# Two cached-attention decode problems on one core: V loads moved from SyncE's to ScalarE's DMA queue, half sums relayed through GpSimd

## The chip, the core and the metric

The kernel runs on one core of a Trainium2 chip. A core has a matmul engine (TensorE, "PE" in the profile, with its weight loads shown apart as "PEld"), an elementwise and reduction engine (VectorE, "DVE"), an activation engine (ScalarE, "ACT"), a general engine (GpSimd, "POOL") and an engine that only issues transfers and waits (SyncE, "SP"). The engines run their own instruction streams and meet at semaphores. Transfers between the large memory (HBM) and the on-chip memory (SBUF) are done by 16 DMA engines; an instruction on SP or ACT starts a transfer ("SPq" and "ACTq" are their issuing sides in the profile). The metric is the device time of one execution in microseconds.

## The reference, cut to what matters

Two independent problems, A and B, are computed and their results concatenated. Each has one query token `x` of width 512, 32 heads of width 128, and a key and a value cache of 16384 positions in bf16; A attends to all positions, B to the last 4096.

```python
def one(x, k_cache, v_cache, wq, wo):            # B first cuts k_cache, v_cache to the last W = 4096 keys
    q = (x @ wq).reshape(B, Sq, 32, 128).transpose(0, 2, 1, 3)
    scores = einsum("bhqd,bhkd->bhqk", q, k_cache) * 128 ** -0.5
    p = softmax(scores, axis=-1)
    o = einsum("bhqk,bhkd->bhqd", p, v_cache)
    return o.transpose(0, 2, 1, 3).reshape(B, Sq, 32 * 128) @ wo     # wo: 4096 x 512
out = concatenate([one(A...), one(B...)], axis=-1)
```

Every key and value is used once, so the bytes are fixed: A's caches are 2 x 134.2 MB, B's parts of them 2 x 33.6 MB, and the four weight matrices 4.19 MB each.

## The kernel before, in words

The work is cut into 20 *loads*. A load is 8.39 MB of K and the same 8.39 MB of V: for A two heads (16 loads, numbers 0 to 15), for B eight heads (4 loads, 16 to 19), in two halves `u` of four heads, each its own transfer of 4.19 MB (`st.U` is 1 for A and 2 for B). One of the 128 partitions receives one contiguous row of HBM from a transfer: 64 KB for an A load, 32 KB for half a B load.

There are two K buffers (`kt`, slots 0 and 1, `_slot(i)` alternates) and one V buffer (`vt`). At the start `vt` holds both query weight matrices, and slot 0 of `kt` small scratch tiles; at the end `vt` takes both output weight matrices, and the last V load (19) goes into the K slot of load 18.

For each load i the engines do this:

- VectorE (`_vector_program`): `mult` multiplies K in place by the query (L292); then `scores(i-1)` sums the 8 remaining partial columns that TensorE left of the load before (L306) into `sc`; then `add` adds the two halves of the head dimension (L300) and signals `s_add`; then `pick(i-1)` cuts the wanted blocks out of the PV product of the load before (L320, L322, L327).
- TensorE (`_tensor_program`): `red(slot)` sums with identity matmuls over the halved head dimension into `red`, four banks, each bank taking one count of `s_add` and giving one of `s_red`; then `pv` multiplies probabilities with V into `acc`, for each half once its probabilities (`s_p`) and its V half are there, giving one count of `s_pv`; then it waits for `pick` and adds the result to `f`. Then comes the next load.
- ScalarE (`_scalar_program`): exponentials of `sc` into `p`, one per head (L216).

So `exp(i)` comes after `scores(i)`, which stands on VectorE behind `mult(i+1)`: the probabilities of a load need the K of the next load. Loads 0 and 1 are cut in four and two parts on VectorE, so that TensorE starts earlier.

SP issues all large transfers, in one written-out order (`_sync_program`, L128): both query weights, K0, then K1, V0, K2, V1, K3, V2 and so on to K19, V18, V19, then the output weights in seven pieces (two of 2.1 MB for A; 2.1, 1.05, 0.52, 0.26, 0.26 MB for B). K(i) first waits until load i-2 has left its slot (`s_red`); V(i-1) until `pv(i-2)` has left `vt` (`s_pv`); V19 until slot of load 18 is free; the output weights until `pv(18)`. ScalarE's queue carries only the two 1 KB rows of x, at the start.

After load 15, and after load 19, `norm` divides by the softmax sums and places the result as columns. After the last norm, TensorE multiplies with A's output weights, then with B's; VectorE and ScalarE convert the output rows, and SP stores them.

Of the kernel before, what the change touches and what calls it, by code (L numbers as in the profile page):

```python
# [19 lines left out]
KEYS = 256  # L20
NB = 4
# [98 lines left out]
def _slot(i):  # L120
    return (i + 1) % 2
# [3 lines left out]
    return cx.p[u][:, 0 : st.keys * st.R].rearrange("p (t g e) -> p t g e", g=st.R, e=4)  # L125


def _sync_program(nc, cx, loads):  # L128
    e = nc.sync
    stA, stB = cx.sts  # L130
    for st in cx.sts:
        st.s_wq.on(e.dma_start(out=st.wq_t, in_=st.wq.rearrange("(p c) f -> p c f", c=st.KC)), 16)

    def kv(st, i, which):
        j = i if st is stA else i - stA.L
        view = st.k_view if which == "k" else st.v_view
        last = which == "v" and i == len(loads) - 1
        for u in range(st.U):
            h0 = (j * st.U + u) * st.R
            k0 = u * st.keys  # L140
            if which == "k":
                out = cx.kt[:, _slot(i), k0 : k0 + st.keys, :]
                sem = cx.s_k[_slot(i)][u]
            elif last:
                out = cx.kt[:, _slot(i - 1), k0 : k0 + st.keys, :]
                sem = cx.s_vlast[u]
            else:
                out = cx.vt[:, k0 : k0 + st.keys, :]
                sem = cx.s_v[u]
            ins = e.dma_start(out=out, in_=view[h0 : h0 + st.R].rearrange("g (i l) d -> i g l d", l=st.keys))  # L150
            sem.on(ins, 16)

    pv = 0
    kv(loads[0], 0, "k")
    for i in range(1, len(loads)):
        if i == 1:
            cx.s_q.wait(e, stA.N // stA.R // 512 + stB.N // stB.R // 512)
        else:
            cx.s_red.wait(e, NB * (i - 1))
        kv(loads[i], i, "k")  # L160
        if i > 1:
            pv += loads[i - 2].U
            cx.s_pv.wait(e, pv)
        kv(loads[i - 1], i - 1, "v")
    n = len(loads)
    cx.s_red.wait(e, NB * (n - 1))
    kv(loads[-1], n - 1, "v")
    cx.s_pv.wait(e, pv + loads[-2].U)
    for st, j0, m, sem in cx.pieces:
        src = st.wo.rearrange("(p j) f -> p j f", j=st.J)  # L170
        sem.on(e.dma_start(out=st.wo_t[:, j0 : j0 + m, :], in_=src[:, j0 : j0 + m, :]), 16)  # L171
    for st in cx.sts:
        st.s_row.wait(e, len(st.out_at))
        cx.s_end.on(e.dma_start(out=cx.out[0, 0:1, st.at : st.at + st.DN], in_=cx.row[0:1, st.at : st.at + st.DN]), 16)
    cx.s_end.wait(e, 32)


def _pool_program(nc, cx):
    e = nc.gpsimd
    e.memset(cx.one[:, :], 1.0)  # L180
    e.memset(cx.ones_col[:, :], 1.0)
    cx.s_own.on(e.memset(cx.ones, 1.0))
    cx.s_own.wait(e, 1)
    cx.s_pool.on(e.affine_select(
        out=cx.ident[:, :], in_=cx.ones[:, 0:P], pattern=[[-1, P]], compare_op=ALU.is_equal,
        fill=0.0, base=0, channel_multiplier=1,
    ))
    w = cx.place_at + 2 * P
    cx.s_pool.on(e.affine_select(
        out=cx.place[:, :], in_=cx.ones[0 : 2 * H, 0:w], pattern=[[1, w]], compare_op=ALU.is_equal,  # L190
        fill=0.0, base=-cx.place_at, channel_multiplier=-cx.n_r,
    ))


def _scalar_program(nc, cx, loads):
    e = nc.scalar
    stA, stB = cx.sts
    for w, st in enumerate(cx.sts):
        st.s_x.on(e.dma_start(out=cx.row[0:1, w * st.D : (w + 1) * st.D], in_=st.x[0, 0:1, :]), 16)
    n = 0  # L200
    for st in cx.sts:
        m = st.N // st.R // 512
        n += m
        cx.s_q.wait(e, n)
        st.s_qall.on(e.copy(st.qall[:, :], cx.red[:, 0:m, :].rearrange("p j f -> p (j f)")))
    cx.s_dve.wait(e, cx.n_off)
    for i, st in enumerate(loads):
        if i == stA.L:
            _orow(e, cx, stA)
        cx.s_sc.wait(e, i + 1)  # L210
        j = i if st is stA else i - stA.L
        for u in range(st.U):
            p = _p_view(cx, st, u)
            for g in range(st.R):
                h = st.f_at + (j * st.U + u) * st.R + g
                ins = e.activation(  # L216
                    out=p[:, :, g, :],
                    in_=cx.sc[:, u * st.keys : (u + 1) * st.keys].rearrange("p (t e) -> p t e", e=4),
                    func=ACT.Exp, scale=SCALE, bias=st.off[:, g : g + 1], accum_out=cx.cs[:, h : h + 1],
                )  # L220
            cx.s_p.on(ins)
    _orow(e, cx, stB)
    w = stB.DN // 2
    stB.s_o.wait(e, 1)
    stB.s_row.on(e.copy(cx.row[0:1, stB.at + w : stB.at + 2 * w], cx.out_ps(stB)[1]))
# [10 lines left out]
def _vector_program(nc, cx, loads):  # L236
# [4 lines left out]
    def did(ins):  # L241
        return own.on(ins)

    for st in cx.sts:
        did(e.memset(st.xb_flat, 0.0))
        did(e.memset(st.sel[:, :], 0.0))
    for acc in cx.acc:
        cx.n_acc = did(e.memset(acc[:, :], 0.0))
    n = did(e.memset(cx.zero, 0.0))
    cx.n_zero = n  # L250
    cx.s_pool.wait(e, 1)
    ident = cx.ident[:, :]
    n = did(e.tensor_reduce(out=cx.rows, in_=ident.rearrange("p (c w) -> p w c", w=H), axis=AX.X, op=ALU.add))
    own.wait(e, n)
# [41 lines left out]

    def add(i, k0, k1, n):
        k = cx.kt[:, _slot(i), k0:k1, :]
        own.wait(e, n)
        cx.s_add.on(e.tensor_tensor(  # L300
            out=k[:, :, 0 : DH // 2], in0=k[:, :, 0 : DH // 2], in1=k[:, :, DH // 2 : DH], op=ALU.add,
        ), NB * (k1 - k0) // KEYS)

    def scores(i):
        cx.s_red.wait(e, NB * (i + 1))
# [30 lines left out]
        st.s_ocs.on(e.tensor_copy(st.oc[:, :], cx.oc_out(st)))  # L336

    for i, st in enumerate(loads):
        n = KEYS // (4, 2)[i] if i < 2 else KEYS
        if i in (0, stA.L):  # L340
            st.s_qall.wait(e, 1)
        for k in range(0, KEYS, n):
            m = mult(i, k, k + n)
            if i and k == 0:
                scores(i - 1)
            add(i, k, k + n, m)
        if i:
            pick(i - 1)
            if i == stA.L:
                norm(stA)  # L350
# [10 lines left out]
def _tensor_program(nc, cx, loads):  # L361
# [1 line left out]
    stA, stB = cx.sts  # L363
    mm = lambda *a, **k: e.matmul(*a, skip_group_check=True, **k)  # L364

    cx.s_pool.wait(e, 2)
    cx.s_dve.wait(e, cx.n_zero)
    mm(cx.f[0 : 2 * H, 0:DH], lhsT=cx.zero[:, 0 : 2 * H], rhs=cx.zero, start=True, stop=True)
    for w, st in enumerate(cx.sts):
        st.s_x.wait(e, 16)  # L370
# [98 lines left out]
@with_exitstack  # L469
def kernel(  # L470
    ctx: ExitStack,
    tc: tile.TileContext,
    A_x: bass.AP,
    A_k_cache: bass.AP,
    A_v_cache: bass.AP,
    A_wq: bass.AP,
    A_wo: bass.AP,
    B_x: bass.AP,
    B_k_cache: bass.AP,
    B_v_cache: bass.AP,  # L480
    B_wq: bass.AP,
    B_wo: bass.AP,
    out: bass.AP,
):
    nc = tc.nc
    SkA = A_k_cache.shape[2]
    SkB = B_k_cache.shape[2]
    WB = min(4096, max(256, SkB // 4))

    cx = _Ctx()  # L490
    cx.out = out
    cx.pe_only = bass.OrderedEngineSet([PE])
    stA = _problem(cx, "A", A_x, A_k_cache, A_v_cache, A_wq, A_wo, 0, SkA, 0)
    stB = _problem(cx, "B", B_x, B_k_cache, B_v_cache, B_wq, B_wo, SkB - WB, WB, A_wo.shape[1])
    cx.sts = (stA, stB)
    loads = [stA] * stA.L + [stB] * stB.L

    ctx.enter_context(tc.tile_critical(sync_engine=mybir.EngineType.SP))
    _alloc(nc, cx, ctx, stA, stB)
    sem = lambda name: _Sem(nc, ctx, name)  # L500
    for st in cx.sts:
        for name in ("wq", "x", "xT", "xb", "qall", "rows", "recip", "orow", "oc", "ocs", "o", "row"):
            setattr(st, f"s_{name}", sem(f"{name}{st.name}"))
    for name in ("q", "red", "pv", "own", "pool", "dve", "sc", "p", "add", "pick", "end"):
        setattr(cx, f"s_{name}", sem(name))
    cx.s_k = [[sem(f"k{a}{u}") for u in range(2)] for a in range(2)]
    for pair in cx.s_k:
        for s in pair:
            s.seen = 0
    cx.s_v = [sem(f"v{u}") for u in range(2)]  # L510
    cx.s_vlast = [sem(f"vl{u}") for u in range(2)]
    J = stA.J
    cx.pieces = [(stA, 0, J // 2, sem("woA0")), (stA, J // 2, J // 2, sem("woA1"))]
    j0 = 0
    for x in (J // 2, J // 4, J // 8, J // 16, J // 16):
        cx.pieces.append((stB, j0, x, sem(f"woB{j0}")))
        j0 += x
    cx.xT = lambda st: cx.oc_ps[:, 0 : st.KC]
    cx.oc_out = lambda st: cx.oc_ps[:, st.J * (st is stB) : st.J * (st is stB) + st.J]
    cx.out_ps = lambda st: [cx.red[r : r + 1, b, 0 : st.DN // len(st.out_at)] for r, b in st.out_at]  # L520

    _sync_program(nc, cx, loads)
    _pool_program(nc, cx)
    _vector_program(nc, cx, loads)
    _scalar_program(nc, cx, loads)
    _tensor_program(nc, cx, loads)


# [28 lines left out]
```

The softmax here doesn't subtract the row's maximum and nothing guards it: scores larger than these inputs give would overflow.

## Time and profile before

| | |
|---|---|
| median of 9 runs | 822.26 us (822.10 to 822.67) |
| the profiled execution's own time | 822.11 us |
| its span, from the first to the last instruction | 820.4 us |
| DMA | 352.42 MB, mean 430 GB/s |
| busy: VectorE | 603.5 us (74%) |
| busy: TensorE matmuls / weight loads | 336.4 us (41%) / 127.1 us (15%) |
| busy: ScalarE | 35.5 us (4%) |
| busy: GpSimd | 1.3 us (0%), all before 2.3 us |

The span is measured inside the device's time, which is 1.7 us longer in this execution. "Busy" counts computing instructions; for DMA the page gives a row of tenths over 40 equal slices of the span, with the rate in each slice under it. A row of the timeline reads: start, duration, engine, line, operation, output<-input, count, and in brackets the idle time of that engine just before and what ended it. "SPq" rows are the moments at which a transfer is issued, not its duration.

### The profile page before, as it was taken

To read this page: it belongs to the slowest core of one execution; us is meant where nothing else is said; L and a number is where in the kernel's file an instruction comes from. 1 tells how busy PE (TensorE), PEld (TensorE's weight loads), DVE (VectorE), ACT (ScalarE), POOL (GpSimd) and SP (SyncE) were. 2 spreads that over 40 slices of the span, in tenths; PEclk is the share of its full clock that TensorE was granted. 3 is DMA by queue.
4 is the path that set the end of the run, shared out by engine and by line. 5 is a ranking of instruction groups with operands and counts; after the bars stand their busy time and mean duration, and the time that the engine had idled before them with its cause. 6 is when DMAs were issued, how large, how long until landed. Compare 5 with 4: busy or idle time off the path is not lost. (4 is left out here: it accounts for less than half of the span.)

```text
span 820.4 us, 5948 instructions
## 1 busy us (share of the span) xinstructions
PE 336.4 (41%) x2149; PEld 127.1 (15%) x2149; DVE 603.5 (74%) x172; ACT 35.5 (4%) x134; POOL 1.3 (0%) x9
## 2 busy tenths in 40 slices
PE   3533347152424343252606071524343352616276
PEld 1211112020101111110202020201111120202022
DVE  2089995959595968768595959595959969696921
ACT  0100000000000000000000000000000001010110
POOL 0000000000000000000000000000000000000000
PEclk9855667595856666756758575858576776857589
DMA  9999999999999999999999999999999999999997
GB/s 384 435 457 412 457 412 457 412 457 413 454 415 454 415 454 412 457 412 457 412 457 413 454 415 451 419 444 425 441 428 423 446 423 423 433 435 435 433 431 317
DMA packets 8223, 352.42 MB, mean 430 GB/s; under 512 B 916, under 2 KB 920, under 8 KB 1304
## 3 DMA queue, kind: packets, MB, share of 16 engines
q1 hardware_dynamic: 8212, 352.33, 99.3%
q8 instruction: 4, 0.07, 0.0%
q14 instruction: 3, 0.02, 0.0%
q10 hardware_dynamic: 4, 0.00, 0.0%
HBM read 352.32 MB, written 0.00 MB: 429 GB/s over the span
## 5 line engine op out<-in xcount | busy, mean ns | idle before, releaser
L292 DVE TENSOR_TENSOR kt<-kt,qallA 128x32768 bf16<-128x32768 bf16 (+2 forms) x20 | 276.2, 13811 | 155.9 <-DMA kt<-in_A_k_cache_dram 155.9
L364 PE MATMUL acc<-vt,p 128*8 128x512 bf16 (+1 forms) x1216 | 110.1, 539 | 354.5 <-PEq L42 354.5
L364 PE MATMUL red<-kt,ident 128*128 x640 | 179.5, 448 | 40.4 <-PEq L42 40.4
L300 DVE TENSOR_TENSOR kt<-kt 128x16384 bf16<-128x16384 bf16 (+2 forms) x24 | 174.3, 7262 | 0.2
L364 PEld LDWEIGHTS acc<-vt,p 128*8 128x8 bf16 (+1 forms) x1216 | 36.6, 112 | 427.1 <-issue 418.2
L364 PEld LDWEIGHTS red<-kt,ident 128*128 128x128 bf16 x640 | 71.1, 111 | 145.3 <-issue 98.0
L292 DVE TENSOR_TENSOR kt<-kt,qallB 128x16384 bf16<-128x16384 bf16 x8 | 69.5, 8691 | 12.9 <-DMA kt<-in_B_k_cache_dram 12.9
L306 DVE TENSOR_REDUCE sc<-red 128x256 f32<-128x2048 f32 x20 | 45.7, 2284 | 8.0 <-PE red L364 8.0
L216 ACT ACTIVATE p<-sc,offA 128x256 bf16<-128x256 f32 x32 | 16.0, 500 | 602.6 <-DVE sc L306 602.6
L364 PE MATMUL f<-s,win 128*32 128x128 f32 x48 | 11.2, 322 | 63.6 <-PEq L42 63.6
L364 PE MATMUL red<-vt,kt 128*128 128x512 bf16 x64 | 18.1, 453 | 7.9 <-DMA vt<-in_A_wq_dram 5.9
L216 ACT ACTIVATE p<-sc,offB 128x128 bf16<-128x128 f32 x32 | 12.4, 388 | 113.2 <-DVE sc L306 113.2
L327 DVE TENSOR_REDUCE s<-acc 128x128 f32<-128x512 f32 x24 | 16.6, 691 | 0.8
L364 PEld LDWEIGHTS f<-s,win 128*32 128x32 f32 x48 | 4.3, 122 | 74.4 <-issue 74.1
L322 DVE TENSOR_TENSOR acc<-acc,maskA 128x512 f32<-128x512 f32 x16 | 11.1, 693 | 0.0
L320 DVE COPY win<-selB 128x32 f32<-128x32 f32 x8 | 1.4, 179 | 12.2 <-PE acc L364 12.2
L364 PEld LDWEIGHTS red<-vt,kt 128*128 128x128 bf16 x64 | 7.1, 113 | 18.6 <-issue 13.7
L364 PE MATMUL red<-vt,ocA 128*1 128x512 bf16 x32 | 7.2, 379 | 0.2 <-DMA vt<-in_A_wo_dram 0.2
L364 PE MATMUL acc<-kt,p 128*16 128x512 bf16 x64 | 5.3, 507 | 4.3 <-PEq L42 4.3
L320 DVE COPY win<-selA 128x32 f32<-128x32 f32 x16 | 2.8, 175 | 5.8 <-PE acc L364 5.8
L216 ACT ACTIVATION_READ_ACCUMULATOR p<-sc,offA 128x1 f32 x32 | 6.0, 187 | 0.0
L355 DVE CAST row<-red 1x512 bf16<-1x512 f32 x1 | 0.7, 679 | 7.2 <-PE red L364 7.2
(47 smaller groups left out, 40.4 us busy)
## 6 DMA issues: line engine op xcount, KB each, us to landing
kt<-in_B_k_cache_dram SPq DMA_DIRECT2D x8, 4096.0 KB, 35.4
vt<-in_B_v_cache_dram SPq DMA_DIRECT2D x6, 4096.0 KB, 28.7
kt<-in_B_v_cache_dram SPq DMA_DIRECT2D x2, 4096.0 KB, 38.3
vt<-in_A_wq_dram SPq DMA_DIRECT2D x1, 4096.0 KB, 12.1
vt<-in_B_wq_dram SPq DMA_DIRECT2D x1, 4096.0 KB, 21.3
vt<-in_A_wo_dram SPq DMA_DIRECT2D x2, 2048.0 KB, 23.3
vt<-in_B_wo_dram SPq DMA_DIRECT2D x1, 2048.0 KB, 29.8
vt<-in_B_wo_dram SPq DMA_DIRECT2D x1, 1024.0 KB, 31.8
```

The source lines that it names most:

```text
L216: ins = e.activation(out=p[:, :, g, :], in_=cx.sc[:, u * st.keys : (u + 1) * st.keys].rearrange("p (t e) -> p t e", e=4), func=ACT.Exp, sc ...
L292: n = did(e.tensor_tensor(out=k, in0=k, in1=q.rearrange("p (o d) -> p o d", o=1).broadcast_to([P, b - a, DH]), op=ALU.mult,))
L300: cx.s_add.on(e.tensor_tensor(out=k[:, :, 0 : DH // 2], in0=k[:, :, 0 : DH // 2], in1=k[:, :, DH // 2 : DH], op=ALU.add,), NB * (k1 - k0) ...
L306: cx.s_sc.on(e.tensor_reduce(out=cx.sc[:, :], in_=cx.red[:, :, :].rearrange("p b (k w) -> p (b k) w", w=W), axis=AX.X, op=ALU.add,))
L320: did(e.tensor_copy(cx.win[u][:, :], st.sel[:, at : at + H]))
L322: n = did(e.tensor_tensor(out=acc, in0=acc, in1=st.mask[:, :].rearrange("p (x o) -> p x o", o=1).broadcast_to([P, 4, DH]), op=ALU.mult,))
L327: cx.s_pick.on(e.tensor_reduce(out=cx.s[u][:, :], in_=acc.rearrange("p x d -> p d x"), axis=AX.X, op=ALU.add,))
L355: stA.s_row.on(e.tensor_copy(cx.row[0:1, 0 : stA.DN], cx.out_ps(stA)[0]))
L364: mm = lambda *a, **k: e.matmul(*a, skip_group_check=True, **k)
```

## The change

Five edits:

- All V loads are issued by ScalarE, on its own DMA queue; SP keeps the weights, the K loads and the output store. The common part becomes the function `_kv`. ScalarE's order for load i is: wait for `pv(i-1)` (for the last load: for `red(18)`, as before; for load 0: nothing), issue V(i), wait for `scores(i)`, exponentials. On SP, K(i) waits as before for `red(i-2)`, and nothing stands between two K loads any more. The output weights wait for `pv(18)` as before.
- The x rows, on ScalarE's queue as before, wait for the first of GpSimd's signals.
- GpSimd takes over from VectorE the zero fills of `xb`, `sel` and `zero`. VectorE and TensorE wait for the third signal of `s_pool`.
- `add` signals `s_half` by one; GpSimd waits for each and adds the 4, 2 or 1 counts to `s_add`. The first `add` of a load waits for `s_sc` instead of VectorE's own counter.
- The critical section is owned by GpSimd instead of SP: the other engines start, and the section ends, through GpSimd.

The output weights stay in the same pieces.

```diff
--- before.py
+++ after.py
@@ -125,47 +125,42 @@
     return cx.p[u][:, 0 : st.keys * st.R].rearrange("p (t g e) -> p t g e", g=st.R, e=4)
 
 
+def _kv(e, cx, loads, i, which):
+    st = loads[i]
+    stA = cx.sts[0]
+    j = i if st is stA else i - stA.L
+    view = st.k_view if which == "k" else st.v_view
+    last = which == "v" and i == len(loads) - 1
+    for u in range(st.U):
+        h0 = (j * st.U + u) * st.R
+        k0 = u * st.keys
+        if which == "k":
+            out = cx.kt[:, _slot(i), k0 : k0 + st.keys, :]
+            sem = cx.s_k[_slot(i)][u]
+        elif last:
+            out = cx.kt[:, _slot(i - 1), k0 : k0 + st.keys, :]
+            sem = cx.s_vlast[u]
+        else:
+            out = cx.vt[:, k0 : k0 + st.keys, :]
+            sem = cx.s_v[u]
+        ins = e.dma_start(out=out, in_=view[h0 : h0 + st.R].rearrange("g (i l) d -> i g l d", l=st.keys))
+        sem.on(ins, 16)
+
+
 def _sync_program(nc, cx, loads):
     e = nc.sync
     stA, stB = cx.sts
     for st in cx.sts:
         st.s_wq.on(e.dma_start(out=st.wq_t, in_=st.wq.rearrange("(p c) f -> p c f", c=st.KC)), 16)
 
-    def kv(st, i, which):
-        j = i if st is stA else i - stA.L
-        view = st.k_view if which == "k" else st.v_view
-        last = which == "v" and i == len(loads) - 1
-        for u in range(st.U):
-            h0 = (j * st.U + u) * st.R
-            k0 = u * st.keys
-            if which == "k":
-                out = cx.kt[:, _slot(i), k0 : k0 + st.keys, :]
-                sem = cx.s_k[_slot(i)][u]
-            elif last:
-                out = cx.kt[:, _slot(i - 1), k0 : k0 + st.keys, :]
-                sem = cx.s_vlast[u]
-            else:
-                out = cx.vt[:, k0 : k0 + st.keys, :]
-                sem = cx.s_v[u]
-            ins = e.dma_start(out=out, in_=view[h0 : h0 + st.R].rearrange("g (i l) d -> i g l d", l=st.keys))
-            sem.on(ins, 16)
-
-    pv = 0
-    kv(loads[0], 0, "k")
+    _kv(e, cx, loads, 0, "k")
     for i in range(1, len(loads)):
         if i == 1:
             cx.s_q.wait(e, stA.N // stA.R // 512 + stB.N // stB.R // 512)
         else:
             cx.s_red.wait(e, NB * (i - 1))
-        kv(loads[i], i, "k")
-        if i > 1:
-            pv += loads[i - 2].U
-            cx.s_pv.wait(e, pv)
-        kv(loads[i - 1], i - 1, "v")
-    n = len(loads)
-    cx.s_red.wait(e, NB * (n - 1))
-    kv(loads[-1], n - 1, "v")
-    cx.s_pv.wait(e, pv + loads[-2].U)
+        _kv(e, cx, loads, i, "k")
+    cx.s_pv.wait(e, sum(st.U for st in loads[:-1]))
     for st, j0, m, sem in cx.pieces:
         src = st.wo.rearrange("(p j) f -> p j f", j=st.J)
         sem.on(e.dma_start(out=st.wo_t[:, j0 : j0 + m, :], in_=src[:, j0 : j0 + m, :]), 16)
@@ -175,8 +170,13 @@
     cx.s_end.wait(e, 32)
 
 
+def _parts(i):
+    return (4, 2)[i] if i < 2 else 1
+
+
 def _pool_program(nc, cx):
     e = nc.gpsimd
+    stA, stB = cx.sts
     e.memset(cx.one[:, :], 1.0)
     e.memset(cx.ones_col[:, :], 1.0)
     cx.s_own.on(e.memset(cx.ones, 1.0))
@@ -190,11 +190,23 @@
         out=cx.place[:, :], in_=cx.ones[0 : 2 * H, 0:w], pattern=[[1, w]], compare_op=ALU.is_equal,
         fill=0.0, base=-cx.place_at, channel_multiplier=-cx.n_r,
     ))
+    for st in cx.sts:
+        e.memset(st.sel[:, :], 0.0)
+        e.memset(st.xb_flat, 0.0)
+    cx.s_pool.on(e.memset(cx.zero, 0.0))
+    n = 0
+    for i in range(stA.L + stB.L):
+        m = _parts(i)
+        for _ in range(m):
+            n += 1
+            cx.s_half.wait(e, n)
+            e.sem_inc(cx.s_add.h, NB // m)
 
 
 def _scalar_program(nc, cx, loads):
     e = nc.scalar
     stA, stB = cx.sts
+    cx.s_pool.wait(e, 1)
     for w, st in enumerate(cx.sts):
         st.s_x.on(e.dma_start(out=cx.row[0:1, w * st.D : (w + 1) * st.D], in_=st.x[0, 0:1, :]), 16)
     n = 0
@@ -207,6 +219,11 @@
     for i, st in enumerate(loads):
         if i == stA.L:
             _orow(e, cx, stA)
+        if i == len(loads) - 1:
+            cx.s_red.wait(e, NB * i)
+        elif i:
+            cx.s_pv.wait(e, sum(s.U for s in loads[:i]))
+        _kv(e, cx, loads, i, "v")
         cx.s_sc.wait(e, i + 1)
         j = i if st is stA else i - stA.L
         for u in range(st.U):
@@ -241,14 +258,9 @@
     def did(ins):
         return own.on(ins)
 
-    for st in cx.sts:
-        did(e.memset(st.xb_flat, 0.0))
-        did(e.memset(st.sel[:, :], 0.0))
     for acc in cx.acc:
-        cx.n_acc = did(e.memset(acc[:, :], 0.0))
-    n = did(e.memset(cx.zero, 0.0))
-    cx.n_zero = n
-    cx.s_pool.wait(e, 1)
+        did(e.memset(acc[:, :], 0.0))
+    cx.s_pool.wait(e, 3)
     ident = cx.ident[:, :]
     n = did(e.tensor_reduce(out=cx.rows, in_=ident.rearrange("p (c w) -> p w c", w=H), axis=AX.X, op=ALU.add))
     own.wait(e, n)
@@ -296,10 +308,13 @@
 
     def add(i, k0, k1, n):
         k = cx.kt[:, _slot(i), k0:k1, :]
-        own.wait(e, n)
-        cx.s_add.on(e.tensor_tensor(
+        if i and k0 == 0:
+            cx.s_sc.wait(e, i)
+        else:
+            own.wait(e, n)
+        cx.s_half.on(e.tensor_tensor(
             out=k[:, :, 0 : DH // 2], in0=k[:, :, 0 : DH // 2], in1=k[:, :, DH // 2 : DH], op=ALU.add,
-        ), NB * (k1 - k0) // KEYS)
+        ))
 
     def scores(i):
         cx.s_red.wait(e, NB * (i + 1))
@@ -336,7 +351,7 @@
         st.s_ocs.on(e.tensor_copy(st.oc[:, :], cx.oc_out(st)))
 
     for i, st in enumerate(loads):
-        n = KEYS // (4, 2)[i] if i < 2 else KEYS
+        n = KEYS // _parts(i)
         if i in (0, stA.L):
             st.s_qall.wait(e, 1)
         for k in range(0, KEYS, n):
@@ -363,8 +378,7 @@
     stA, stB = cx.sts
     mm = lambda *a, **k: e.matmul(*a, skip_group_check=True, **k)
 
-    cx.s_pool.wait(e, 2)
-    cx.s_dve.wait(e, cx.n_zero)
+    cx.s_pool.wait(e, 3)
     mm(cx.f[0 : 2 * H, 0:DH], lhsT=cx.zero[:, 0 : 2 * H], rhs=cx.zero, start=True, stop=True)
     for w, st in enumerate(cx.sts):
         st.s_x.wait(e, 16)
@@ -495,13 +509,13 @@
     cx.sts = (stA, stB)
     loads = [stA] * stA.L + [stB] * stB.L
 
-    ctx.enter_context(tc.tile_critical(sync_engine=mybir.EngineType.SP))
+    ctx.enter_context(tc.tile_critical(sync_engine=mybir.EngineType.Pool))
     _alloc(nc, cx, ctx, stA, stB)
     sem = lambda name: _Sem(nc, ctx, name)
     for st in cx.sts:
         for name in ("wq", "x", "xT", "xb", "qall", "rows", "recip", "orow", "oc", "ocs", "o", "row"):
             setattr(st, f"s_{name}", sem(f"{name}{st.name}"))
-    for name in ("q", "red", "pv", "own", "pool", "dve", "sc", "p", "add", "pick", "end"):
+    for name in ("q", "red", "pv", "own", "pool", "dve", "sc", "p", "add", "half", "pick", "end"):
         setattr(cx, f"s_{name}", sem(name))
     cx.s_k = [[sem(f"k{a}{u}") for u in range(2)] for a in range(2)]
     for pair in cx.s_k:
```

## The prediction

> **What bounds the kernel now.** I read the slices first, then the stretches of one load, the timeline of one load, and the end. The DMA row and the queue table of the page:
>
> ```profile
> DMA  9999999999999999999999999999999999999997
> GB/s 384 435 457 412 457 412 457 412 457 413 454 415 454 415 454 412 457 412 457 412 457 413 454 415 451 419 444 425 441 428 423 446 423 423 433 435 435 433 431 317
> ...
> q1 hardware_dynamic: 8212, 352.33, 99.3%
> ```
>
> The 16 DMA engines are never empty, so only the bytes count until the last piece. The same in two stretches of one A load each (columns: stretch, length, busy time of PE, PEld, DVE, ACT, POOL with counts, TensorE clock, DMA share, GB/s):
>
> ```profile
> 140.20:178.80 38.60, 15.31 (x103) 5.90 (x102) 29.41 (x7) 1.09 (x4) 0.00 (x0) 0.69 1.00 435
> 178.80:217.40 38.60, 14.08 (x101) 5.49 (x100) 29.39 (x6) 1.09 (x4) 0.00 (x0) 0.73 1.00 435
> ```
>
> 38.6 us for 16.78 MB is 434.7 GB/s: 19.3 us for one K or V load, and VectorE's 29.4 us fit inside. The page counts packets too: one per partition row explains them (32 A transfers, 16 of B, 9 of weights, 128 each, is 7296; 57 x 16 small ones for semaphores and four of the output make 8212). So a packet is 64 KB for A, 32 KB for B, 16 KB for A's output weights. Now one load's order, from the timeline:
>
> ```profile
> 178.78 17.23 DVE L292 TENSOR_TENSOR kt<-kt,qallA 128x32768 bf16<-128x32768 bf16 x1 [9.16 <-DMA kt<-in_A_k_cache_dram]
> ...
> 198.24 0.51 ACT L216 ACTIVATE p<-sc,offA 128x256 bf16<-128x256 f32 x1 [37.51 <-DVE sc L306]
> ...
> 199.63 4.89 PE L364 MATMUL acc<-vt,p 128*8 128x512 bf16 x64 [19.88 <-PEq L42]
> ...
> 204.57 0.54 SPq L150 DMA_DIRECT2D vt<-in_A_v_cache_dram  x1
> ...
> 218.08 0.54 SPq L150 DMA_DIRECT2D kt<-in_A_k_cache_dram  x1
> ```
>
> K(i+1) lands at 178.8. `pv(i)` starts 20.8 us later, V(i+1) is issued at +25.8, K(i+3) at +39.3, after `red(i+1)`. K(i+1) landed, V(i) follows at +19.3, K(i+2) at +38.6: each issue comes 13 to 19 us ahead of its turn in the one queue. That cover is what two queues must replace. Last, the end:
>
> ```profile
> 754.20 1.18 SPq L150 DMA_DIRECT2D kt<-in_B_v_cache_dram  x2
> ...
> 800.64 0.18 DVE L320 COPY win<-selB 128x32 f32<-128x32 f32 x1 [1.03 <-PE acc L364]
> ...
> 803.54 3.61 PE L364 MATMUL red<-vt,ocA 128*1 128x512 bf16 x16
> ```
>
> V19 is issued at 754.2, when `red(18)` is done. Its PV ends at 800.6, some 16 us before the last weights land; the chain of waits ends on those weights, so all of load 19's arithmetic is hidden.
>
> **What the Trainium skill says.** "DMA: Bandwidth & Descriptors", Issuing engines are not separate DMA queues: transfers of different issuers run on the same 16 DMA engines and interleave. The trace agrees: B's x row, on ScalarE's queue, is issued 0.5 us after the first weights and read by TensorE at 7.09, while those weights land at 13.2. The same page, Queues, rings and completion order: each DMA engine takes turns between rings packet by packet. The trace of before doesn't show the turns between two large streams; I take it. Where 436 GB/s comes from, there: a ceiling of 435.2 GB/s; the trace has 434.7, so two queues can't gain rate.
>
> **The change part by part.** *Owner, fills, relay, x.* GpSimd's present 128x384 bf16 fill takes 0.41 us (1.08 ns per element of a partition); the moved fills have 1024 + 2048 + 128 and two small ones, 3.6 us, so the third signal comes at 2.2 + 3.6 = 5.8 us. VectorE's preparations (4.05 to 5.38) move behind it, to about 7.2. The x rows are issued after the first signal, at about 1.9 and 2.4 instead of 0.97 and 1.52; with B's present 5.5 us both are there by 8, and copies of 0.8 and 1.3 us end by about 11. The first query weights land at 13.2: hidden, with 2 us of reserve, and 9.7 us more behind that, as K0 lands at 43.7 and the last query copy ends at 34.5. Price if the cover went: the excess alone. The relay adds two semaphore steps between `add` and `red`, bound 0 to 0.3 us; but `red` waits for `pick`, 1.5 us after `add` (206.72 to 208.2), so nothing. The owner: bound -0.2 to +0.3 us at both ends, taken as 0.2.
>
> *V on its own queue, loads of A.* Rules from the rows above: V(i+1) is issued 5.5 us after the later of V(i)'s landing and K(i+1)'s landing + 20.8; K(i+3) at the later of K(i+1)'s landing + 39.3 and `pv(i)`'s end + 11.6 (667.81 to 679.46, timeline). 1.3 us pass from issue to first byte (the first 3.5 us moved 0.53 MB, so data began at 2.3), about 1 us to landing. Two loads in flight get half the rate each. One pair of loads: K6 starts at 229.0, when V4 still needs 8.85 of its 19.3 us. V4 ends at 246.7; K6, alone for the next 7.8 us, then shares with V5 (from 254.5) and ends at 259.8. V5 is alone until K7 starts at 266.5, ends at 286.4; K7 at 297.2. Next comes V6 at 294.3, and the pattern repeats every 77.2 us for two loads, 38.6 each: no idle DMA. So A's body costs nothing, as the gap of one stream lies inside the other.
>
> At the start it isn't covered. V0 is issued at 34.2 and shares with K0, which lands at 47 instead of 43.7; K2 has drained at 98.8 and V1, behind `pv(0)`, starts at 99.8; V1 drains at 119.1 and K3, behind `red(1)`, starts at 122.0: 1.0 + 2.9 us. Where A turns into B another 1.5 us are lost (V16 also stands behind A's `orow`).
>
> *The end.* This is what decides. On ScalarE, V19 now stands behind the exponentials of load 18, which wait for VectorE's `mult` of K19. Following the recurrence, K19's halves land at 751 and 764; `mult` ends at 775.4, `scores` at 777.6, eight exponentials (3.3 us) at 780.9, and only then is V19 issued, 27 us later than now. V18 has drained at 779.8, V19 starts at 782.2: 2.4 us idle. The idle time in all is 1.0 + 2.9 + 1.5 + 2.4 = 7.8 us.
>
> `pv(18)` ends at 786.6 (V18 landed 780.7), and the weights start at 787.9. V19 has 5.7 of its 19.3 us done; the other 13.6 share with them. By packets, 32 KB against 16 KB, V19 has two thirds: 20.4 us, landing at 809.2 instead of 796.4. What was hidden now follows: the last half of `pv(19)` 3.65 (wait until 812.9), `pick` to A's weights 2.9 (800.64 to 803.54), A's matmuls 2 x 3.61, B's 4.3 (group of the page), conversion and store 2.9: 812.9 + 2.9 + 7.2 + 4.3 + 2.9 = 830.2, and 1 us for hand-overs that the recurrence has (it gives 821 for the kernel before, 820.4 in the profile), with the owner 0.2: 831.4. The execution is 1.7 us longer than its span, 833.1, and the median 0.15 above the profiled execution: **833 us**, 11 us (1.3%) slower.
>
> **Rivals.** *Equal bytes* (or V19 favoured less): V19's remaining 13.6 us take 27.2, landing at 816; all behind it moves by 6.8: 840. For: nothing in the trace shows the turns. With the queues uneven by half again in the body (V three shares, K two), K comes late, DMA drains in some loads, and the recurrence gives 843 to 848.
>
> *Lost rate.* Two streams of 64 KB rows could run below 434.7 GB/s; at 2% less, 810 us of data become 826, and the end 848. Against: the rate equals the ceiling that the skill states, whether K or V flows.
>
> *Served in order of issue, so no change.* If the DMA engines drained one queue's transfer before the other's, K and V would alternate as now, V19 would be issued after the exponentials at 772.7 of the present timeline, ahead of V18's landing at 777, and the weights at 781.45, all in time: 822.4, not slower. It decides where V18 still has over 1.3 us to run at V19's issue and the weights are served wholly behind V19. Against: B's x row overtook the weights.
>
> *A milder end*: V18 still running when V19 is issued (K ahead of V), and V19 favoured 3 to 1: it lands at 805, all behind it 4 us earlier, 828.
>
> **How the numbers follow.** Packet turns 0.52 (829 to 837); equal or uneven shares 0.22 (838 to 848); milder end 0.12 (825 to 829); lost rate 0.08 (846 to 870); order of issue or something else that leaves no loss 0.06, of which 0.04 no change and 0.02 a gain from start-up. 827 to 846 leaves out 2 in 10: most of the lost rate, the no-change cases and parts of the milder end and of uneven shares. Slower by over 0.2% (about what a measurement of this kernel can tell from no change, 1.6 us): 0.94; within: 0.04; faster: 0.02.
>
> **What would show it.** In the profile after: V transfers issued by ACTq, each with a landing time of some 30 us; stretches of two A loads (77.2 us) with DMA share still 1.00 at 435 GB/s; dips at about 99 and 120, near 682 and 780; the last V issue behind the last exponentials of load 18, near 781; and at the end a chain of waits that runs through V19's landing, `acc`, `pick` and A's output weights' matmuls, with TensorE no longer waiting for weights. Wrong would be: A's stretches longer than 38.6 us (rate or uneven turns), or a chain that still ends on the weights' transfer (order of issue). A late first query matmul, after 13.3, would show that the fills or x came too late.

## The result, and the profile after

The changed kernel takes 842.78 us (median of 10 runs), the kernel before 822.37 us (30 runs): 1.0233 times as long, 95% interval 1.0218 to 1.0247. The forecast was 833 us, range 827 to 846. The runs also spread: 835.7 to 850.7 us after, 822.0 to 823.0 before. The ratio leaves out the two slowest of the ten runs, which lie more than 1.5% above the fastest. The profiled execution took 839.86 us, its span is 837.8 us.

First the page of the kernel after, the slices and the queues:

```profile
DMA  9999999999999999999999999999999999999997
GB/s 385 461 404 413 391 401 401 451 448 404 401 451 429 422 451 426 426 451 401 441 413 429 435 385 413 438 447 404 401 451 426 440 419 439 429 426 430 418 429 304
...
q1 hardware_dynamic: 4756, 184.55, 51.2%
q10 hardware_dynamic: 3460, 167.78, 46.9%
```

The row of tenths looks as before; the two lines of queues don't. Packets of both queues took 98.1% of 837.8 us, 821.9 us, against 99.3% of 820.4, 814.7 us. So two things happened: the same bytes took some 7 us more of the DMA engines' time, and the engines were empty for longer. The trace's packet records give both. Idle of the 16 engines, averaged over them, from the first packet to the last is 11.4 us instead of 1.8. And 7.9 us are packets' time above the usual one (2.418 us for a 64 KB packet) instead of 1.0. Together 9.6 + 6.9 = 16.5 us, which is what the last packet is later (833.3 instead of 816.8). The span is 17.4 us longer, so 0.9 us are left for the arithmetic at the end.

Where, by stretches (columns as in the prediction; the DMA share counts a packet where it starts, so that a short stretch can be off by a tenth or more). First the kernel before, in two short stretches and over some twelve loads of A, then the kernel after:

```profile
218.00:225.00 7.00, 0.05 (x1) 0.00 (x0) 7.00 (x1) 0.00 (x0) 0.00 (x0) 0.84 0.82 356
...
495.00:500.00 5.00, 0.00 (x0) 0.00 (x0) 5.00 (x1) 0.00 (x0) 0.00 (x0) 0.50 0.97 419
...
140.00:618.00 478.00, 180.80 (x1185) 68.01 (x1183) 367.14 (x73) 13.12 (x48) 0.00 (x0) 0.68 1.00 434
```

```profile
218.00:225.00 7.00, 4.45 (x52) 1.61 (x45) 3.27 (x4) 0.00 (x0) 0.00 (x0) 0.85 0.79 300
225.00:300.00 75.00, 25.75 (x195) 9.79 (x193) 57.38 (x12) 2.18 (x8) 0.00 (x0) 0.73 1.00 433
...
495.00:500.00 5.00, 2.73 (x34) 0.75 (x22) 2.56 (x4) 0.00 (x0) 0.00 (x0) 0.84 0.76 262
...
140.00:618.00 478.00, 167.88 (x1183) 64.00 (x1184) 357.19 (x76) 13.12 (x48) 0.00 (x0) 0.70 0.99 426
```

Over most of a load the rate is nearly unchanged (433 GB/s). It collapses in short stretches, near 220 and 497 here (also near 577), where one queue runs dry before the other has begun. The rate of such a short stretch is rough, as 356 GB/s before in 218 to 225 shows; the packet records are the better evidence. By them the DMA engines idled 1.3 us around 222, 2.2 us around 497 and 1.1 us around 577, where the kernel before has none. In all the idle is 4.3 us at the start (80 to 125), 5.1 us in A's body (125 to 620), 0.2 us near 792; the rest, near the first and the last packets, is as before.

One load in the timeline, to be held against the one in the prediction:

```profile
223.19 17.22 DVE L304 TENSOR_TENSOR kt<-kt,qallA 128x32768 bf16<-128x32768 bf16 x1
...
242.65 0.51 ACT L233 ACTIVATE p<-sc,offA 128x256 bf16<-128x256 f32 x1 [35.03 <-DVE sc L321]
...
253.77 5.50 PE L379 MATMUL acc<-vt,p 128*8 128x512 bf16 x64 [21.69 <-PEq L42]
259.32 0.54 ACTq L146 DMA_DIRECT2D vt<-in_A_v_cache_dram  x1
```

PV (the matmuls of `pv`) now starts 30.6 us after its K, not 20.8: it waits for V. V's last packet had ended at 250.93 by the packet records, and the landing signal came at 253.63, 2.7 us later; before, this step took 0.3 us for a load of A. The next V is issued at 259.32, right at the end of PV, so ScalarE's own work holds nothing up, and its first packet starts 3.0 us after that. From the last V packet to the next first one 11.4 us pass; I call this V's gap. When it opened, the K load in flight still had 12.1 us to run: 0.7 us to spare. Over the loads 2 to 13 the packet records give a gap of 10.0 to 13.8 us, K's rest of 9.7 to 14.5 us, and a spare of -0.9 to 2.3 us. It is negative after loads 3, 10 and 12, and these are the three stretches near 220, 497 and 577.

The end, and the chain that ended last:

```profile
787.19 2.28 DVE L321 TENSOR_REDUCE sc<-red 128x256 f32<-128x2048 f32 x1
...
790.41 0.54 ACTq L146 DMA_DIRECT2D kt<-in_B_v_cache_dram  x1
...
797.80 0.81 SPq L166 DMA_DIRECT2D vt<-in_A_wo_dram  x2
...
820.18 2.18 PE L379 MATMUL acc<-kt,p 128*16 128x512 bf16 x32 [0.72 <-PEq L42]
```

```profile
825.13 0.26 PE oc_ps L379 x4
825.39 9.65 PE red L379 x92
835.04 0.02 issue
835.07 0.42 DVE row L373
```

V19 is issued after the scores of load 18, lands at 820.0 beside the weights, and from there the chain of arithmetic runs to the end: TensorE no longer waits for weights, its 92 recorded matmuls with them stand in one piece. It is a close race, though. The last weights land at 833.5; before, the span ended 3.3 us after that landing, which here would be 836.8, and V19's chain ends at 837.8.

### The profile page after: what moved, and what is told of

Same layout as the page of the kernel before. It is cut to its first block, busy times and chain, and to the rows that moved or that the text cites. A ratio compares the mean times of both kernels' runs of the same rounds, so it can differ in the third digit from the quotient of the medians.

```text
span 837.8 us, 5952 instructions
## 1 busy us (share of the span) xinstructions
PE 323.2 (39%) x2149; PEld 123.0 (15%) x2149; DVE 604.2 (72%) x167; ACT 35.5 (4%) x134; POOL 4.3 (1%) x14
## 5 line engine op out<-in xcount | busy, mean ns | idle before, releaser
L379 PE MATMUL red<-kt,ident 128*128 x640 | 166.7, 416 | 46.4 <-PEq L42 46.2
L379 PEld LDWEIGHTS red<-kt,ident 128*128 128x128 bf16 x640 | 66.7, 104 | 142.2 <-issue 94.1
L233 ACT ACTIVATION_READ_ACCUMULATOR p<-sc,offB 128x1 f32 x32 | 6.0, 187 | 0.0
## 6 DMA issues: line engine op xcount, KB each, us to landing
vt<-in_B_v_cache_dram ACTq DMA_DIRECT2D x6, 4096.0 KB, 20.9
```

Source lines behind the costliest of these rows:

```text
L233: ins = e.activation(out=p[:, :, g, :], in_=cx.sc[:, u * st.keys : (u + 1) * st.keys].rearrange("p (t e) -> p t e", e=4), func=ACT.Exp, sc ...
```

## The experiments

My theory after this comparison is that the whole loss comes from the second queue: V's queue runs empty for some 11 us per load, and K's queue has just about as much left at that moment. I call this the gap theory. The rivals are the relay, the fills or the late x; two interleaved streams that simply move less; and the packet size. The diffs below are cut to the lines that matter. Idle times and other readings of packets come from one profiled execution of each run.

**All edits but the queue.** The V loads go back to SP in the old order; all else stays as changed.

```diff
 (in _scalar_program)
-        _kv(e, cx, loads, i, "v")
 (in _sync_program, behind each K load)
+        if i > 1:
+            cx.s_pv.wait(e, sum(st.U for st in loads[: i - 1]))
+        _kv(e, cx, loads, i - 1, "v")
```

> The change with the V loads back on SP, in the old order between the K loads; owner, fills, relay and x stay as changed. Hand-over theory (the whole loss comes from the second DMA queue): 822.4 us, within 0.5 us of before, DMA share 1.00 in every A load. Rival (the relay or the fills delay the start or each load): up to 0.3 us for each of 20 loads or 1 us at the start, 823 to 829, and DMA never empty less than before.

822.19 us, ratio 0.9999 (0.9990 to 1.0008). The queue line of its page is that of before:

```profile
q1 hardware_dynamic: 8212, 352.33, 99.4%
```

Owner, fills, relay and x cost nothing that can be measured.

**The queue alone.** The kernel before, with only the V loads issued by ScalarE, each behind its wait, as in the change.

```diff
 (in _scalar_program of the kernel before)
+        if i == len(loads) - 1:
+            cx.s_red.wait(e, NB * i)
+        elif i:
+            cx.s_pv.wait(e, sum(s.U for s in loads[:i]))
+        _kv(e, cx, loads, i, "v")
```

> The kernel before with the V loads alone moved to ScalarE's queue; no other edit. Hand-over theory: the same as the whole change, 836 to 851 us with a median near 842, as V and K hand over late. Rival (the relay, the fills or the late x rows cause part of it): less, 825 to 835.

842.04 us, ratio 1.0248 (1.0208 to 1.0288). The two runs together settle which part of the change costs. How the loss is made up differs from one execution to the next: here A's body has only 1.5 us of idle, and the last packet is 14.7 us later than before, but the span still 17.2 us longer.

**Smaller packets, and their own price.** Each A load in two transfers of 32 KB rows, on the change and on the kernel before.

```diff
+            for c in range(2):
+                sem.on(e.dma_start(out=out[:, c * m : (c + 1) * m, :], in_=src[:, :, c * m : (c + 1) * m, :]), 16)
```

> The change with each A load cut into two transfers, so that a packet is 32 KB instead of 64 KB. In the changed kernel's trace a transfer that starts beside a running one sends its first packet 4.8 us after its issue, two packets of 2.42 us. Late-join theory: this falls to about 2.4 us, DMA's idle time and the slow packets of A to less than half (16.5 us to about 8), while the packets themselves cost 0.3% more (2 us): about 836. Rival (two interleaved streams are slower whatever their packets, or PV and the waits alone make the gap): 842 to 845.

> The kernel before with each A load cut into two transfers, on the one queue: the price of the smaller packets alone. A 64 KB packet takes 2.418 us, two of 32 KB 2.426 us, on 268 MB (617 us): 2 us more, 824.4, by both theories.

823.40 us on one queue (ratio 1.0012, 1.0005 to 1.0019), so the price is 1 us. On two queues 845.99 us, ratio 1.0291 (1.0273 to 1.0308): longer, not shorter. My reading of the late start was wrong. By the packet records the landing signal did nearly halve, from 2.7 to 1.55 us beside a running stream, but the time from issue to first packet beside a running stream stayed mostly between 3.6 and 4.3 us. V's gap fell from 11.3 to 9.8 us in the mean, and yet the idle rose from 11.4 to 16.1 us. Why it rose is not settled.

**V later.** Four small copies on ScalarE ahead of each A load of V, 2.6 us by the trace.

```diff
         elif i:
             cx.s_pv.wait(e, sum(s.U for s in loads[:i]))
+            if i < stA.L:
+                for _ in range(4):
+                    cx.s_lag.wait(e, cx.s_lag.on(e.copy(cx.p[1][:, :], cx.p[1][:, :])))
         _kv(e, cx, loads, i, "v")
```

> The change with four small copies on ScalarE, some 2.5 us in all, between the free signal and the issue of each A load of V (they change nothing that is used). Gap theory: V's gap, already near K's reserve, exceeds it in each load, so nearly each of 15 loads loses another 1.5 to 2.5 us: 865 to 880. Rival (K in flight covers the gap and the rate is what is lost): 842 to 846.

866.86 us, ratio 1.0562 (1.0522 to 1.0602): 24 us on top of the change. Its page shows where most of it lies:

```profile
DMA  9998999999999989999999999999999999999994
GB/s 389 436 438 356 426 389 438 438 390 438 389 435 380 426 374 429 389 438 389 392 435 389 438 389 438 389 438 389 438 389 407 430 430 434 436 435 431 420 427 190
```

Nearly every A load has a slice at 389 GB/s beside one at 438, and the packet records show about 1.5 to 1.9 us of idle in each load from the third on: V's gap is now 13 us, K's rest 12.1, so the spare is -0.9 to -1.2 us in every load. The last packet ends 19.3 us later than in the change. Nothing hides a further wait of V; its gap is at the limit of what K covers. The rest of the 24 us, 4.6 in this execution, is arithmetic behind V19's landing, where TensorE had a lower granted clock (0.71 instead of 0.98).

**Transfers only.** K on one queue and V on the other, in halves, each waiting only for the transfer before it in its own buffer; no arithmetic, no output weights, and zeros stored as output.

```diff
+    if sem.n:
+        sem.wait(e, sem.n)
+    sem.on(e.dma_start(out=dst, in_=src), 16)
```

> Transfers only, without any arithmetic and without the output weights: the query weights, then all K on SP's queue and all V on ScalarE's, in halves of 4.19 MB, each half waiting only for the landing of the transfer before it in its own buffer, so that both queues always have work. It writes zeros. 343.9 MB. Gap theory: the two interleaved streams run at the one-queue rate (434.7 GB/s less 0.3% for 32 KB packets), 794 us plus some 6 at start and end: 798 to 803, no slow packets. Rival (interleaving costs rate): 1 to 2% more, 806 to 816.

800.22 us. Its page:

```profile
q1 hardware_dynamic: 6052, 176.17, 51.2%
q10 hardware_dynamic: 5760, 167.77, 48.7%
HBM read 343.93 MB, written 0.00 MB: 431 GB/s over the span
```

The queues are busy for 99.9% of the span, and no packet after the start takes longer than usual. From 50 to 780 us the rate is 434 GB/s, against 433 with A's loads in such packets on one queue, in the run above. Interleaving as such costs nothing: the lost-rate rival falls.

**V handed over by halves.** Each half of A's V has its own semaphore, PV takes and frees it by itself, and ScalarE issues the next half at once, so that its queue stays filled.

```diff
+            for h in (range(2) if st is stA else (u,)):
+                cx.s_pv.wait(e, 2 * (i - 1) + h + 1) if i else None
+                cx.s_v[h].on(e.dma_start(out=cx.vt[:, h * m : (h + 1) * m, :], in_=src), 16)
 (in pv of _tensor_program)
+                if t % 32 == 0:
+                    if t:
+                        ins.then_inc(cx.s_pv.h, 1)
+                    sems[u + t // 32].take(e, 16)
```

> The change with V handed over by halves: each A load of V is two transfers with their own semaphores, PV takes and frees each half by itself, and the half of the next load is issued as soon as its own half is free. So ScalarE's queue need not run empty between two loads. Gap theory (the loss in the body arises because V's queue is empty for about 11 us per load, signal 2.7 + PV 5.5 + join 3, against about 12 us that K has left then; where K runs out first, DMA idles and the next stream starts slowly): DMA idle in the body goes to nearly zero, slow packets with it, and 3 to 5 us are left of the start and the end: 826 to 831. Rival (two interleaved streams simply move less): 840 or more, as two streams then run together even longer.

833.11 us, ratio 1.0123 (1.0101 to 1.0145): half of the loss is gone, somewhat less than I expected. Idle at the start and in A's body fell from 9.4 to under 1 us. What is left sits elsewhere: 4.2 us of idle near 782, where V18 has drained and V19 is issued only at 784.5, the mechanism that the prediction named for the end; 5.3 us of slow packets, some 4 more than before; and 2.2 us more between the last packet and the end.

**The last V back on SP.** On top of the halves, V19 is issued behind K19 on SP, ahead of the weights.

```diff
+    cx.s_red.wait(e, NB * (len(loads) - 1))
+    _kv(e, cx, loads, len(loads) - 1, "v")
     cx.s_pv.wait(e, 2 * (len(loads) - 1))
```

> The kernel with V by halves, and in addition the last V load back on SP, behind K19 and ahead of the output weights, as before the change. The prediction's account of the end: no idle near 780 (3.8 us in the kernel with halves, where V19 is issued only after the scores of load 18), V19 lands earlier than the weights by 19 us of data, the end falls from 5.8 us after the last packet to 3.6: about 6 us less than with halves alone, 825 to 828. Rival (the end is bound by the weights in any case): 832 to 834.

835.04 us (833.0 to 840.8), ratio 1.0174 (1.0131 to 1.0216): no gain, where I expected 6 us. The idle is gone, 2.1 us in all, about that of the kernel before, and the last packet ends at 819.6, but the span is 831.3. The timeline of its end:

```profile
791.99 3.59 PE L384 MATMUL acc<-vt,p 128*16 128x512 bf16 x32 [5.43 <-PEq L42]
...
798.07 8.25 PE L384 MATMUL red<-kt,ident 128*128 x32 [0.18 <-PEq L42]
806.36 2.29 DVE L326 TENSOR_REDUCE sc<-red 128x256 f32<-128x2048 f32 x1 [9.21 <-PE red L384]
810.62 5.32 PE L384 MATMUL acc<-kt,p 128*16 128x512 bf16 x64 [4.30 <-PEq L42]
```

V18 lands at 791.9, as V19 now shares with it; with the halves alone it landed at 783.6, before the change at 778.3. `red(19)` stands on TensorE behind `pv(18)`, and all that follows stands behind `red(19)`: from V18's landing to the end of the span 39.5 us. The earlier transfer was delayed for the later one, and the earlier one was needed first. So even with the DMA engines filled, this kernel with two queues is slower than before.

**V18 held until K19 has landed.** From the landing of K19 to the end of the span it was 61 to 66 us in the runs so far; I took K19 for the cause and gave it the DMA engines alone.

```diff
+        if i == len(loads) - 2:
+            for sem in cx.s_k[_slot(i + 1)]:
+                sem.wait(e, sem.n)
```

> The kernel with V by halves and the last V load on SP, and in addition V18 issued only once K19 has landed. In the runs so far the span ended 60.8 to 66 us after K19's landing: 758.6 before, 776.9 with the change, 772.6 with halves, 770.1 with the last V on SP, where DMA idled only 2 us in all and the time still was 833 to 841. Theory: at the end the arithmetic behind K19 sets the time, and K19 is late because it shares with V18. K19 alone lands near 762, the span ends near 823 to 826, the time is 825 to 829. Rival (the end is set by V19 or the weights): V19 and the weights come no earlier than in the kernel that this one is made from, so 833 to 838.

841.43 us, ratio 1.0225 (1.0209 to 1.0241): a miss, outside what my theory and its rival gave. K19 landed at 766.1, 4.0 us earlier, but V18, issued at 766.15 and shared with V19, at 800.3, 8.5 us later, and the span ended 39.5 us after that, as in the run before. So V18, not K19, sets the end in these two runs. Holding V18 back also left the DMA engines idle for 3.4 us.

**K later.** By the gap theory a K load that starts later has more left when V's gap comes. So SP does idle increments of a semaphore, 58 ns each by the trace, ahead of each A load of K from the third on.

```diff
             cx.s_red.wait(e, NB * (i - 1))
+            if i < stA.L:
+                for _ in range(32):
+                    e.sem_inc(cx.s_lag.h, 1)
         _kv(e, cx, loads, i, "k")
```

> The change with 32 idle semaphore increments on SP between the wait for red and the issue of each A load of K from the third on, some 1.5 us (the trace will tell). Gap theory: V's gap, about 11.4 us, is covered while K still has data when V returns; a K load that starts later still has more of it, so a delay of K makes the kernel faster: DMA idle in the body from 5 to about 1 us, and 834 to 840 us. Rivals (lost rate, or any longer wait costs): 842 to 860.

> The same with 96 increments, some 4.5 us. Gap theory: K's gap (about 11.5 us) grows to 15 and lies inside V's run of 27 us; idle in the body stays near zero: 833 to 840. Rival (a longer wait costs): 850 to 880.

840.99 us (ratio 1.0223, 1.0204 to 1.0242) with 32, 847.44 us (1.0284, 1.0249 to 1.0320) with 96. The first lies 1 us outside what I expected, the second is a miss in time. The packet records explain most: idle in A's body went from 5.1 to 2.0 and 4.0 us, but at the start, where K2 and K3 are late as well, from 4.3 to 6.8 and 9.8 us. So I left the start out:

```diff
-            if i < stA.L:
+            if 5 < i < stA.L:
```

> The change with 32 idle increments (1.9 us, as measured) before the issue of K6 to K15 only, so that the start is as in the change. With the delay from K2 on, DMA idle in the body fell from 5.1 to 2.0 us but rose by 2.7 at the start. Gap theory: idle in the body 1 to 2 us, start as in the change, 836 to 841, not slower than the change's 842.8. Rival (each longer wait costs): 845 to 862.

839.90 us (838.7 to 843.1), ratio 1.0222 (1.0206 to 1.0238). A wait of 1.9 us added to ten loads made nothing slower, where 2.6 us added to V cost 24, and that is what the gap theory asks for. In the loads 4 to 13, where K is late, the spare is now 1.2 to 2.1 us, never negative, and idle in the body fell to 0.7 us; over the twelve loads the rate is 432 GB/s, against 426 with the change and 434 before:

```profile
140.00:618.00 478.00, 181.17 (x1210) 68.49 (x1210) 359.87 (x77) 13.11 (x48) 0.00 (x0) 0.70 1.00 432
```

The fall of the idle alone would prove little, as the run with the queue alone had 1.5 us without any delay; the spare, and V later against K later, are the stronger evidence. That the kernel became faster isn't shown: the intervals of 1.0222 and 1.0233 overlap. The profile of this run says why so little came of it. The last packet ends 5.5 us earlier than with the change and V19 lands 4.2 us earlier, at 815.8, but still beside the weights, and the span ends 20.8 us after that instead of 17.7. These 3.1 us are TensorE's: its granted clock behind V19's landing was 0.83 here and 0.98 there, PV's last 32 matmuls took 3.6 us instead of 2.2, and the same 92 matmuls with weights 11.34 us instead of 9.65.

## Why the prediction was right, and where it was not

*The bound, and the sign.* These were right. There was no rate to gain and one queue was always filled; the loss is the second queue's, and the other edits are hidden (0.9999). The third signal of GpSimd came at 5.2, foreseen at 5.8. B's x, which I had put at 8, was read at 10.65; the first query matmul started at 13.56 against 13.28 before. That is after the 13.3 that I had named as a sign of late fills or x, but it follows the weights' landing (13.42), not x, whose copies ended at 12.3. The reserve was 1 us rather than 2. The reserve behind that, from the last query copy to K0's landing, is 9.2 us in the lines of before, not 9.7; nothing hangs on it.

*The size: in part luck.* In my sum the span grew by 11.0 us: 7.8 of idle DMA engines and 3.2 of arithmetic exposed behind the last transfers. Measured were 17.4 us: 16.5 of the DMA engines and 0.9 of exposed arithmetic. The main account, 829 to 837 us, doesn't contain the measured 842.8. It lies in the range because that was drawn out to 846 for equal or uneven shares, and these did not occur. A's loads took 39.2 us each on average (K from 147.7 to 618.1, twelve loads) instead of 38.6, which I had named as a sign of a lost rate or uneven turns; it was neither.

*"So A's body costs nothing": wrong, and the largest error.* The terms of V's gap were mis-sized. Landing was put at about 1 us and the start at 1.3, measured in a trace where no second stream ran beside: 7.8 us of gap with PV. Beside a running stream the landing signal takes 2.7 us and the first packet mostly 2.3 to 5.5: the measured gap is 11.3 us in the mean. The other side was mis-sized too: K follows V's issue by 10.4 us in most loads, not 11.6. With these the reserve is gone and A loses 5.1 us of idle in this execution. The trace of before had the hint: B's x row took 5.5 us beside the weights, and I used that number for x alone. For the signal the Trainium skill has a reason, in "DMA: Bandwidth & Descriptors", Queues, rings and completion order: the increment of a semaphore lands only after every earlier write of its DMA engine, across its queues. The traces of A's loads agree: 0.3 us with one queue, 2.7 us beside 64 KB packets of the other queue (2.42 us each), 1.55 us beside 32 KB packets (1.21 us each). That it is this and nothing else isn't shown: with one queue most of B's loads took 0.7 to 1.6 us and most pieces of the output weights 1.4 to 1.7.

*Slow packets: not foreseen.* The first packets of a stream that starts when the engines have just drained take mostly 3.0 to 3.3 us instead of 2.42 (near 223). Such packets make up most of the 6.9 us. They are absent where no queue drains (transfers only); the time above the usual is 3.0 us with the last V on SP and 11.5 us with V later. What makes them slow is open.

*The start, and A to B.* At the start 3.9 us of idle were foreseen and 4.3 measured. Where A turns into B 1.5 were foreseen and none measured.

*The end.* The chain was right: K19, scores, V19's issue, V19's landing beside the weights, then TensorE to the end. Two links were off. V19 is issued at 790.41, while the exponentials of load 18 still run (to 792.7), not behind them; it follows the scores' signal. And V18 was still running, to 793.7, so the foreseen 2.4 us of idle did not come; idle of this kind, 4.2 us, is seen in the run with halves. The share of two thirds holds: beside V19 the engines moved 77 packets of 16 KB and 79 of 32 KB from 805 to 814 us, and the first weights' piece, 2.1 MB or 4.8 us alone, took 12.9 us, 37%. From V19's landing to the end it was 17.7 us, not 22. I had put no term for TensorE's clock, which a transfer at the end had hidden before: behind V19's landing the granted clock was 0.98 here, but 0.81 with halves and 0.82 with the queue alone, and there the same steps took 20.8 and 20.9 us. Their weights' matmuls show it (the run with halves; 9.65 us above):

```profile
819.39 11.34 PE red L383 x92
```

All of the chain is later, mostly by what the start and the body lost: K19 landed at 776.9 instead of 764.1, V19 at 820.0 instead of 809.2, the span ended at 837.8 instead of 831.4.

*The rivals.* The turns by packet are as taken: two A loads alternate one to one (32 and 32 packets from 240 to 250 us; V0 took 36.1 us for 19.3 us of data beside K0 and K1). "Lost rate" falls by the run of transfers only. "Order of issue" falls with the result. The milder end did not come.

What stays open: why smaller packets raised the idle; what the first packets after a drain wait for; and where the spread of 15 us between runs comes from. Between the profiled executions the arithmetic at the end differs by some 3 us, with the granted clock, and A's idle by another 3.6 (5.1 and 1.5 us); of the other runs the times alone are known.

## What to carry to other kernels

In this kernel the transfers shared engines that were already full. A second queue added no rate; it replaced a written order by equal turns, and the transfer needed first paid for the one needed later. Before moving a stream to its own queue, add up that queue's empty time per turn (landing signal and start beside a running stream, not alone, plus the work that frees the buffer) and hold it against what the other queue has left at that moment; where the two are equal, a further wait is no longer hidden. And look at which arithmetic was hidden behind the last transfers: filling the DMA engines again did not bring the time back, since the order at the end had changed, and arithmetic that is no longer hidden made the time depend on TensorE's granted clock too.

## What the runs showed of the hardware

- From the last packet of an A load to its landing signal 0.3 us pass with one queue, 1.55 us beside 32 KB packets of a second queue, 2.7 us beside 64 KB packets.
- From the issue to the first packet 1.0 to 1.3 us pass into empty engines; beside a running stream mostly 2.3 to 5.5 us, and halving the packets did not halve this.
- Two queues that both stay filled move as much as one: 434 GB/s with 32 KB packets, against 433 on one queue.
- Two large streams take turns packet by packet: 32 packets to 32 with 64 KB each, 77 to 79 with 16 KB against 32 KB, so that the bytes go by the size of the packets.
- The first packets after the engines drained take mostly 3.0 to 3.3 us instead of 2.42.
- A transfer on ScalarE's queue was issued at 790.41 us, while exponentials ahead of it in the program still ran, to 792.7.
- In the eight profiled executions that end alike, the time from V19's landing to the end of the span went with the granted clock of that stretch: 17.7 us at 0.98, 18.1 at 0.96, 20.3 to 20.9 at 0.81 to 0.84, 22.3 at 0.71.
- Increments of a semaphore on SP follow each other every 58 ns.
- With one queue 30 runs lie within 1.1 us, with two queues ten runs lie within 15 us.
